# Hashed attention and a maxout feed-forward: the first batch's scores and transposes as products on 32 columns

## The chip, the cores and the metric

The kernel runs on one core of one Trainium2 chip. The metric is the device time of one execution in microseconds (us). The kernel before takes 295.62 us, the median of 3 runs (295.52 to 295.69).

## The reference

For each of 4 batches and 8 heads (768 positions, 64 dimensions), queries and keys are hashed to 6 sign bits with `proj`; a query attends only to keys of its own bucket; the result goes through a feed-forward layer that takes the maximum of three products.

```python
q_bits = (np.einsum('bhsd,dk->bhsk', q, proj) > 0)      # 6 bits, k likewise
mask = q_bucket[:, :, :, None] == k_bucket[:, :, None, :]
scores = np.where(mask, scale * (q @ k.T), -1e9)
attn = np.exp(scores - max) ; attn = attn / (attn.sum(-1) + 1e-9)
x = (attn @ v)                                          # to [3072 tokens, 512]
h = np.maximum(np.maximum(x @ w1, x @ w2), x @ w3)      # [3072, 768]
out = h @ w_out                                         # [3072, 512]
```

## The kernel before

**Units.** The 32 (batch, head) pairs are worked two heads at a time: 16 head pairs `pi`, 4 to a batch. A head pair has 12 units: 2 halves of the queries (`qh`, 384 each) times 3 parts of the keys (`kp`) times 2 heads. There are 192 units `u`, 48 to a batch (`UPB`), 6 to a query half (`UPG`), 12 to a head pair (`UPP`). The core's program is one loop over `u`; every engine gets its instructions in the order in which this loop issues them, and works them off in that order. Nothing is scheduled by a tool: the order is written out by hand.

**Preparing a head pair.** `prep_groups(pi)` gives four `tgroup`s, each of which turns one head of q or k round: three transposes of 128x128 fp32 on TensorE into the PSUM tile `mp` (L150), from where VectorE copies them to `T` (L158, L160) and, for pairs 2 to 7, the odd half of the positions also to `S` (L166, L168). Then `hashes` multiplies `T` with the projection (`bp`, L205: four fp32 products, each on 32 columns), VectorE makes bits of it (L208), and four small transfers on GpSimd's queue put the bits below the data in `S` (L214). `even` copies the other half (L217, GpSimd). So `S` has 70 rows, 64 of data and 6 of bits, and one product gives score and bucket match together. Pair 0 has its own path (`odd_first`, `hash_first`, `bits_first`), ordered by the list `first`. In the loop, a fill (one `tgroup` or one `hashes`) is issued at `u` = 2 to 6 and then at every odd `u` up to 60: 24 `tgroup`s of pairs 1 to 6, 6 `hashes`, and two `tgroup`s of pair 7.

**Scores.** `scores(u)` issues two products of 70 rows on 128 columns (keys) by 384 queries into `sc` (L301), which has two buffers, and ScalarE takes the exponential into one of 14 tiles `AT` (L304).

**Values.** `values_part` multiplies `AT` with `v` (`av`, L327, 8 products on 32 columns for one part of the keys) and with ones for the sums (`sm`, L332, 4 products on 32 columns). In the first batch one such group of 12 follows every second unit; `av` has one buffer. After a query half, `values` has VectorE take the result out (`sv`, `avs`, `ys`, L343 to L346).

**The chain of a head pair.** `normalize` collects the sums by a transfer (`dd`, SP queue, L367), inverts them on VectorE (`rr`, L370 and L372), writes them to DRAM (`rd`, SP queue, L373), reads them back spread over the partitions (`rb`, SP queue, L377), and multiplies on GpSimd into `xT` (L381). The list that it returns says how many units later each step is issued: invert, spread, scale. The steps wait in `steps` and are issued at the head of a loop body, in the order of their unit.

**Feed-forward.** `ffn_groups(b)` is issued from unit 13 of the next batch on (`FFN_AT`), about one group per unit: products with the weights (`l`, L244, four `jc` for the four head pairs of the batch), the maximum on VectorE (L249, L251), and the second product (L260). So the first batch, u = 0 to 60, has no feed-forward in it, and that of the last batch stands alone at the end of the program.

**Loads.** q and k of pair `pi + 2` are loaded when the preparation of `pi` begins, v of the next pair at the head of each pair (`load_v`, L122) and cast at its unit 10 (L125), weights in 15 parts at the units of `WEIGHTS_AT`, all on GpSimd's queue (L411 to L418).

Of the kernel before, what the change touches and what calls it, by code (L numbers as in the profile page):

```python
# [17 lines left out]
def kernel(  # L18
# [12 lines left out]
    nc = tc.nc  # L31
    B, H, S, D = q.shape
    NBITS = proj.shape[1]
    P = 128
    NCH = S // P

    HALF = S // 2
# [4 lines left out]
    NPAIR = B * HPAIR  # L42
# [10 lines left out]
    EPS = 2.0 ** -60  # L53

    AHEAD = 6
    ODD_LATE, ODD_PSUM = 1, 8
    LAG = 1

    konst = ctx.enter_context(tc.tile_pool(name="konst", bufs=1))
# [25 lines left out]

    def load_proj():
        for par in range(2):
            rows = slice(par * D, (par + 1) * D)
            nc.scalar.dma_start(pst[rows, :], proj[:, :])
            nc.vector.tensor_copy(pj[rows, 1 + par, 0:NBITS], pst[rows, :])  # L90
            nc.vector.tensor_copy(pj[rows, 0, par : 2 * NBITS : 2], pst[rows, :])

    bias_t = konst.tile([P, 1], FP32, name="bias_t")
    nc.vector.memset(bias_t[:], EXP_BIAS)
# [38 lines left out]
    def prep_groups(pi):  # L133
# [9 lines left out]
        def tgroup(side, hd):  # L143
            def go():
                if not st:
                    begin()
                mp = ms_ps.tile([P, 512], FP32, tag="ms", name="mp")
                n = natural[pi][side]
                for i in range(CH2):
                    nc.tensor.transpose(mp[:, i * P : (i + 1) * P], n[:, hd, 2 * i * D : (2 * i + 2) * D], iden[:])  # L150
                o = st["T2"][:, side, hd, :]
                if pi == 0 and (hd, side) != (0, 1):
                    if side == 0:
                        nc.scalar.mul(o, mp[:, 0:HALF], QS)
                    else:
                        nc.scalar.copy(o, mp[:, 0:HALF])
                elif side == 0:
                    nc.vector.tensor_scalar(out=o, in0=mp[:, 0:HALF], scalar1=QS, scalar2=None, op0=AluOp.mult)  # L158
                else:
                    nc.vector.tensor_copy(o, mp[:, 0:HALF])  # L160
                if pi == 0:
                    nc.gpsimd.tensor_copy(st["S"][0:D, side, hd, 0, :], o[0:D])
                elif ODD_LATE < pi < ODD_PSUM:
                    o, i_ = st["S"][0:D, side, hd, 1, :], mp[D : 2 * D, 0:HALF]
                    if side == 0:
                        nc.vector.tensor_scalar(out=o, in0=i_, scalar1=QS, scalar2=None, op0=AluOp.mult)  # L166
                    else:
                        nc.vector.tensor_copy(o, i_)  # L168
            return go
# [53 lines left out]
        if pi == 0:  # L223
            k0, k1 = (1, 0, 0, P), (1, 1, 0, P)
            early = (k0, k1, (0, 0, 0, HALF), (1, 0, P, HALF), (1, 1, P, HALF))
            return [tgroup(1, 0), tgroup(0, 0), tgroup(1, 1), lambda: odd_first(0), lambda: hash_first(0), tgroup(0, 1),
                    lambda: bits_first(0, early), lambda: scores(0), lambda: hash_first(1, (1,)), lambda: odd_first(1),
                    lambda: bits_first(1, early[:2]), lambda: scores(1), lambda: scores(2), lambda: hash_first(1, (0,)),
                    lambda: bits_first(1, early[2:]), lambda: bits_first(0, ((0, 1, 0, HALF),)),
                    lambda: bits_first(1, ((0, 1, 0, HALF),))]  # L230
        odds = [odd(1), odd(0)]
# [55 lines left out]
    UPB = NU // B  # L287
    UPG = NCH
    UPP = 2 * UPG
    WEIGHTS_AT = (2, 4, 6, 8) + tuple(range(12, 48, 5)) + (63, 67, 71)  # L290
    FFN_AT = 13
    FIRST = 2
    PAIRS_AT = UPB + UPP
# [2 lines left out]
    def scores(u):  # L296
        pi, qh, kp, hd = units[u]
        th = trans[pi]
        sc = sc_ps.tile([P, 2, 512], FP32, tag="sc", name="sc")
        for j in range(2):  # L300
            nc.tensor.matmul(sc[:, j, 0:HALF], th[0:KR, 1, hd, j, kp * P : (kp + 1) * P],  # L301
                             th[0:KR, 0, hd, qh, :], start=True, stop=True)
        at = at_tiles[u % NAT]
        nc.scalar.activation(at[:, :, 0:HALF], sc[:, :, 0:HALF], ActFn.Exp, bias=bias_t[:], scale=SCALE)  # L304

# [46 lines left out]
    def normalize(pi, q0, nq):  # L352
# [27 lines left out]
        def scale(i):  # L380
            return lambda: nc.gpsimd.tensor_mul(xt[:, jj, (q0 + i) * HALF : (q0 + i + 1) * HALF],  # L381
                                                avs[:, q0 + i, :], rb[:, i, :])

        gather()
        if nq == 1:
            return [(4, invert), (6, spread), (8, scale(0))] if pi == NPAIR - 1 else [(7, invert), (11, spread), (15, scale(0))]
        at = (8, 13, 18) if jj < 2 else (6, 9, 14)
        return [(at[0], invert), (at[1], spread)] + [(at[2], scale(i)) for i in range(nq)]

    with tc.manual_schedule():  # L390
# [6 lines left out]
        cast_v = {0: load_v(0, nc.sync)}  # L397
        load(2, nc.sync)
        first = prep_groups(0)
        for g in first:  # L400
            g()

        prep, hash_ready, late, ffn, steps = [], [], [], [], []
        f_credit = 0.0
# [3 lines left out]
        for u in range(NU):  # L408
            pi = units[u][0]
            b, ub = divmod(u, UPB)  # L410
            if u % UPP == 0 and pi + 1 < NPAIR:  # L411
                cast_v[pi + 1] = load_v(pi + 1, nc.gpsimd)
            if u == FIRST:
                cast_v[0]()
            if u % UPP == 10 and pi + 1 < NPAIR:
                cast_v[pi + 1]()
            if u in WEIGHTS_AT:
                nc.gpsimd.dma_start(*weight_parts.pop(0))  # L418
# [77 lines left out]
```

## Time and profile before

| What | us |
|---|---|
| Median of 3 runs | 295.62 |
| The profiled execution, its own time | 295.93 |
| Its span in the profile | 294.0 |
| TensorE (PE) busy | 285.0, 97% of the span |
| ScalarE (ACT) busy | 195.4, 66% |
| VectorE (DVE) busy | 188.7, 64% |
| GpSimd (POOL) busy | 139.7, 48% |
| Stretch from u = 8 to the feed-forward, 18.02 to 69.43: PE | 49.51 of 51.41 |
| Same stretch: ACT, DVE, POOL | 46.13, 40.44, 44.38 |

TensorE's products are pipelined: a product is shown for about 0.17 us longer than it keeps the next one from starting, and products on different groups of 32 columns run side by side. So a row such as "0.51 us, x8" is the time from the first start to the last end, and the cost of a group on the path is read from its start to the start of the next group. PEld is the loading of the stationary operand. The granted clock of TensorE is full nearly throughout.

### The profile page before, as it was taken

To read this page: it belongs to the slowest core of one execution; us is meant where nothing else is said; L and a number is where in the kernel's file an instruction comes from. 1 tells how busy PE (TensorE), PEld (TensorE's weight loads), DVE (VectorE), ACT (ScalarE), POOL (GpSimd) and SP (SyncE) were. 2 spreads that over 40 slices of the span, in tenths; PEclk is the share of its full clock that TensorE was granted. 3 is DMA by queue.
4 is the path that set the end of the run, shared out by engine and by line. 5 is a ranking of instruction groups with operands and counts; after the bars stand their busy time and mean duration, and the time that the engine had idled before them with its cause. 6 is when DMAs were issued, how large, how long until landed. Compare 5 with 4: busy or idle time off the path is not lost.

```text
span 294.0 us, 6792 instructions
## 1 busy us (share of the span) xinstructions
PE 285.0 (97%) x2592; PEld 159.7 (54%) x2592; DVE 188.7 (64%) x419; ACT 195.4 (66%) x238; POOL 139.7 (48%) x187
## 2 busy tenths in 40 slices
PE   8898999998999999999999999999999999999994
PEld 4454454444656566555665556555655555555551
DVE  2886977788865387736667377654757167657480
ACT  3779899886847956797785965888696956010202
POOL 2765799889806556291905636090801702220000
PEclk9999999999999999999999999999999999999999
DMA  6877666864952733336222522315011211230203
GB/s 206 266 166 204 164 169 186 233 161 123 271 158 63 233 97 116 107 67 261 83 88 64 176 107 59 101 48 175 9 54 59 102 49 41 64 134 2 107 0 108
DMA packets 20276, 35.90 MB, mean 122 GB/s; under 512 B 6080, under 2 KB 12484, under 8 KB 20244
## 3 DMA queue, kind: packets, MB, share of 16 engines
q0 software_dynamic: 8992, 19.81, 25.2%
q1 hardware_dynamic: 10948, 15.52, 16.3%
q8 instruction: 20, 0.33, 0.5%
q10 hardware_dynamic: 304, 0.13, 0.2%
q14 instruction: 12, 0.10, 0.1%
HBM read 31.46 MB, written 6.39 MB: 129 GB/s over the span
## 4 chain that ended last, share of the span: by engine, by line
PE 90%; DMA 3%; DVE 2%; ACT 2%; issue 1%; POOL 0%; SPq 0%; ACTq 0%; POOLq 0%; DVEq 0%
PE l L244 32%; PE sc L301 21%; PE av L327 11%; PE l L260 11%; PE mp L150 6%; PE sm L332 5%; PE bp L205 3%; DMA rb<-rd 2%; ACT AT L304 2%; PE wm L393 1%; PE bp L191 1%; DMA rd<-rr 0%; DVE S L168 0%; POOL xT L381 0%; DVE rr L372 0%
## 5 line engine op out<-in xcount | busy, mean ns | idle before, releaser
L304 ACT ACTIVATE AT<-sc,bias_t 128x768 f16<-128x768 f32 x192 | 168.9, 903 | 53.9 <-PE sc L301 48.3
L244 PE MATMUL l<-xT,w_sb 128*128 128x384 f16 x576 | 110.0, 326 | 1.0 <-POOL xT L381 1.0
L301 PE MATMUL sc<-S 70*128 70x384 bf16 x384 | 93.8, 327 | 1.8 <-ACT AT L304 1.5
L244 PEld LDWEIGHTS <-w_sb 128*128 128x128 f16 x576 | 55.9, 97 | 36.3 <-issue 1.5
L214 POOL DMA_DIRECT2D S<-bits x58 | 32.9, 570 | 86.0 <-DVE bits L208 55.5
L251 DVE TENSOR_TENSOR ht<-ht,l 128x384 f16<-128x384 f16 x96 | 52.9, 551 | 18.1 <-PE l L244 13.5
L301 PEld LDWEIGHTS <-S 70*128 70x128 bf16 x384 | 33.8, 98 | 41.7 <-issue 20.2
L327 PE MATMUL av<-AT,vo 128*32 128x385 f16 x768 | 48.3, 330 | 1.0 <-DVE avs L344 0.7
L381 POOL TENSOR_TENSOR xT<-avs,rb 128x384 f16<-128x384 f32 x32 | 31.5, 1000 | 31.1 <-DMA rb<-rd 31.1
L249 DVE CAST ht<-l 128x384 f16<-128x384 f32 x48 | 26.5, 553 | 25.3 <-PE l L244 24.4
L274 ACT COPY osb<-l 128x512 f32<-128x512 f32 x23 | 13.4, 585 | 35.0 <-PE l L260 35.0
L260 PE MATMUL l<-wout_sb,ht 128*128 128x512 f16 x144 | 36.5, 379 | 0.0
L332 PE MATMUL sm<-AT,ones 128*32 128x384 f16 x384 | 32.7, 324 | 0.0
L327 PEld LDWEIGHTS <-vo 128*32 128x32 f16 x768 | 17.3, 95 | 20.0 <-issue 10.9
L160 DVE COPY T<-mp 128x384 f32<-128x384 f32 x31 | 17.0, 549 | 13.7 <-PE mp L150 13.6
L158 DVE TENSOR_SCALAR T<-mp 128x384 f32<-128x384 f32 x30 | 16.6, 554 | 12.7 <-PE mp L150 11.3
L217 POOL CAST S<-T 64x1536 bf16<-64x1536 f32 x15 | 22.1, 1476 | 0.0
L260 PEld LDWEIGHTS <-ht 128*128 128x128 f16 x144 | 14.0, 97 | 12.7 <-DVE ht L251 0.2
L344 DVE TENSOR_SCALAR avs<-av,sv 128x384 f32<-128x384 f32 x32 | 19.8, 618 | 1.6
L346 DVE TENSOR_SCALAR ys<-sm 128x384 f32<-128x384 f32 x32 | 17.5, 548 | 0.0
L343 DVE TENSOR_SCALAR sv<-av 128x1 f32<-128x1 f32 x32 | 5.1, 158 | 18.3 <-PE av L327 17.8
L150 PE MATMUL mp<-iden,knat 128*128 128x128 f32 x96 | 16.2, 277 | 0.0
(45 smaller groups left out, 191.4 us busy)
## 6 DMA issues: line engine op xcount, KB each, us to landing
out_dram<-osb SPq DMA_DIRECT2D x23, 256.0 KB
vnat<-in_v_dram POOLq DMA_DIRECT2D x15, 384.0 KB, 4.8
knat<-in_k_dram POOLq DMA_DIRECT2D x13, 384.0 KB, 4.3
qnat<-in_q_dram POOLq DMA_DIRECT2D x13, 384.0 KB, 5.1
rb<-rd SPq DMA_DIRECT2D x24, 192.0 KB
w_sb<-in_moe_w_dram POOLq DMA_DIRECT2D x12, 192.0 KB, 4.7
rb<-rd SPq DMA_DIRECT2D x16, 96.0 KB
S<-bits POOLq DMA_DIRECT2D x58, 9.0 KB, 2.4
```

Source lines behind the costliest of these rows:

```text
L150: nc.tensor.transpose(mp[:, i * P : (i + 1) * P], n[:, hd, 2 * i * D : (2 * i + 2) * D], iden[:])
L214: eng.dma_start(st["S"][D:KR, side, hd, :, :], bits[p0 : p0 + 2 * NBITS, :])
L217: nc.gpsimd.tensor_copy(st["S"][0:D, :, :, 0, :], st["T2"][0:D])
L244: nc.tensor.matmul(ps[:, 0:HALF], w_sb[wi][:, jc, fb * P : (fb + 1) * P], xb[:, jc, hf * HALF : (hf + 1) * HALF], start=(jc == 0), stop=(j ...
L249: nc.vector.tensor_copy(hts[fb][:], ps[:, 0:HALF])
L251: nc.vector.tensor_tensor(out=hts[fb][:], in0=hts[fb][:], in1=ps[:, 0:HALF], op=AluOp.max)
L260: nc.tensor.matmul(st2["l2"][:, 0:DM], hts[fb][:, tb * P : (tb + 1) * P], wout_sb[:, fb, :], start=(fb == 0), stop=(fb == NFB - 1))
L301: nc.tensor.matmul(sc[:, j, 0:HALF], th[0:KR, 1, hd, j, kp * P : (kp + 1) * P], th[0:KR, 0, hd, qh, :], start=True, stop=True)
L304: nc.scalar.activation(at[:, :, 0:HALF], sc[:, :, 0:HALF], ActFn.Exp, bias=bias_t[:], scale=SCALE)
L327: nc.tensor.matmul(av[p0 : p0 + 32, 0 : HALF + 1], vones[pi][:, hd, d0 : d0 + 32], ats[hd][:, c % 2, 0 : HALF + 1], start=(c == 0), stop=( ...
L332: nc.tensor.matmul(sm[32 * t : 32 * t + 32, 0:HALF], ones[:, :], ats[hd][:, half, 0:HALF], start=(s == 0), stop=(s == CH2 - 1))
L381: return lambda: nc.gpsimd.tensor_mul(xt[:, jj, (q0 + i) * HALF : (q0 + i + 1) * HALF], avs[:, q0 + i, :], rb[:, i, :])
```

## The change

Four things change, and all but the last two bear on the first batch alone.

1. For u = 3 to 60, `scores` issues eight products on 32 columns each (`M = 32`) in place of two on 128: four groups of 32 keys, in four column groups, for each of the two halves.
2. For pairs 1 to 6 (`TILED` = 7), a `tgroup` issues twelve fp32 products with the identity, each of 32 columns by 128, in place of three transposes.
3. The chain of a pair: for the third pair of a batch the steps stand at 7, 11, 16 units in place of 6, 9, 14; for the fourth pair the scale stands at 14 in place of 15 (the last pair of all keeps 4, 6, 8).
4. Loads: v is loaded two pairs ahead, at unit 8 of a pair, and cast at unit 4 of the pair before its own (unit 10 at the start); the first 12 weight parts go out from unit 4 to 52 in place of 2 to 47. At the start, the second half of the copies of the projection moves behind the first `tgroup`, and one hash of pair 0 moves ahead of the scores of unit 2.

```diff
-    ODD_LATE, ODD_PSUM = 1, 8
+    ODD_LATE, ODD_PSUM, TILED = 1, 8, 7
...
     def load_proj():
         for par in range(2):
-            rows = slice(par * D, (par + 1) * D)
-            nc.scalar.dma_start(pst[rows, :], proj[:, :])
-            nc.vector.tensor_copy(pj[rows, 1 + par, 0:NBITS], pst[rows, :])
-            nc.vector.tensor_copy(pj[rows, 0, par : 2 * NBITS : 2], pst[rows, :])
+            nc.scalar.dma_start(pst[par * D : (par + 1) * D, :], proj[:, :])
+
+    def place_proj(par):
+        rows = slice(par * D, (par + 1) * D)
+        nc.vector.tensor_copy(pj[rows, 1 + par, 0:NBITS], pst[rows, :])
+        nc.vector.tensor_copy(pj[rows, 0, par : 2 * NBITS : 2], pst[rows, :])
...
                 for i in range(CH2):
-                    nc.tensor.transpose(mp[:, i * P : (i + 1) * P], n[:, hd, 2 * i * D : (2 * i + 2) * D], iden[:])
+                    if 0 < pi < TILED:
+                        for g in range(4):
+                            c0 = 2 * i * D + 32 * g
+                            nc.tensor.matmul(mp[32 * g : 32 * g + 32, i * P : (i + 1) * P], n[:, hd, c0 : c0 + 32],
+                                             iden[:], start=True, stop=True)
+                    else:
+                        nc.tensor.transpose(mp[:, i * P : (i + 1) * P], n[:, hd, 2 * i * D : (2 * i + 2) * D], iden[:])
...
-                    lambda: bits_first(1, early[:2]), lambda: scores(1), lambda: scores(2), lambda: hash_first(1, (0,)),
+                    lambda: bits_first(1, early[:2]), lambda: scores(1), lambda: hash_first(1, (0,)), lambda: scores(2),
...
-    WEIGHTS_AT = (2, 4, 6, 8) + tuple(range(12, 48, 5)) + (63, 67, 71)
+    WEIGHTS_AT = (4, 8, 13, 17, 21, 26, 30, 34, 39, 43, 47, 52, 63, 67, 71)
...
+        M = 32 if FIRST < u < UPB + FFN_AT else P
         for j in range(2):
-            nc.tensor.matmul(sc[:, j, 0:HALF], th[0:KR, 1, hd, j, kp * P : (kp + 1) * P],
-                             th[0:KR, 0, hd, qh, :], start=True, stop=True)
+            for p0 in range(0, P, M):
+                nc.tensor.matmul(sc[p0 : p0 + M, j, 0:HALF], th[0:KR, 1, hd, j, kp * P + p0 : kp * P + p0 + M],
+                                 th[0:KR, 0, hd, qh, :], start=True, stop=True)
...
-            return [(4, invert), (6, spread), (8, scale(0))] if pi == NPAIR - 1 else [(7, invert), (11, spread), (15, scale(0))]
-        at = (8, 13, 18) if jj < 2 else (6, 9, 14)
+            return [(4, invert), (6, spread), (8, scale(0))] if pi == NPAIR - 1 else [(7, invert), (11, spread), (14, scale(0))]
+        at = (8, 13, 18) if jj < 2 else (7, 11, 16)
...
         first = prep_groups(0)
-        for g in first:
+        place_proj(0)
+        for i, g in enumerate(first):
             g()
+            if i == 0:
+                place_proj(1)
...
-            if u % UPP == 0 and pi + 1 < NPAIR:
-                cast_v[pi + 1] = load_v(pi + 1, nc.gpsimd)
+            ahead = 1 if u == 0 else 2 if u % UPP == 8 else NPAIR
+            if pi + ahead < NPAIR:
+                cast_v[pi + ahead] = load_v(pi + ahead, nc.gpsimd)
             if u == FIRST:
                 cast_v[0]()
-            if u % UPP == 10 and pi + 1 < NPAIR:
+            if u % UPP == (4 if pi else 10) and pi + 1 < NPAIR:
                 cast_v[pi + 1]()
```

The text of the prediction counts lines by the kernel before.

## The prediction

> **What bounds the kernel now.** I read the page's busy times, the chain that ended last, the groups by line, and then the timeline of the first batch and of the tail.
>
> ```profile
> span 294.0 us, 6792 instructions
> PE 285.0 (97%) x2592; PEld 159.7 (54%) x2592; DVE 188.7 (64%) x419; ACT 195.4 (66%) x238; POOL 139.7 (48%) x187
> ...
> PE 90%; DMA 3%; DVE 2%; ACT 2%; issue 1%; POOL 0%; SPq 0%; ACTq 0%; POOLq 0%; DVEq 0%
> ...
> L301 PEld LDWEIGHTS <-S 70*128 70x128 bf16 x384 | 33.8, 98 | 41.7 <-issue 20.2
> ```
>
> PE bounds the program: 97% busy, 90% of the chain. What the change gains or loses in the first batch reaches the end, since from 71 to 259 us PE is never idle. The last line shows score weights idle for "issue" (20.2 us in 48 places): nothing that another engine did was missing. The timeline of PE shows where:
>
> ```profile
> 44.39 0.85 PE L205 MATMUL bp<-T,pj 128*32 128x384 f32 x8
> 45.18 0.50 PE L301 MATMUL sc<-S 70*128 70x384 bf16 x2
> 45.61 0.51 PE L327 MATMUL av<-AT,vo 128*32 128x385 f16 x8
> 45.95 0.34 PE L332 MATMUL sm<-AT,ones 128*32 128x384 f16 x4
> 46.22 0.50 PE L301 MATMUL sc<-S 70*128 70x384 bf16 x2
> 46.55 0.49 PE L150 MATMUL mp<-iden,knat 128*128 128x128 f32 x3
> 46.88 0.49 PE L301 MATMUL sc<-S 70*128 70x384 bf16 x2
> 47.30 0.51 PE L327 MATMUL av<-AT,vo 128*32 128x385 f16 x8
> ```
>
> From start to start: sc to mp 0.33, mp to sc 0.33, sc to av 0.42, av to sm 0.34, sm to sc 0.27. Four products side by side cost 0.16 to 0.17 a round (av: 2 rounds; three value groups in a row at 28.11, 28.61, 29.11 stand 0.49 apart). So each passage between 32 and 128 columns costs extra: sc to av 0.42-0.33 = 0.09, sm to sc 0.27-0.165 = 0.10, and the hash (0.79 for two passes of 0.33) about 0.1 at its end. ACT is close behind, 46.13 of 51.41 us, with 0.78 to 0.80 for one exponential when it is not kept waiting, against 1.69/2 = 0.85 per unit on PE.
>
> ```profile
> 51.79 0.44 DVE L372 RECIPROCAL rr<-rr 32x48 f32<-32x48 f32 x1
> ...
> 52.46 0.62 DVE L344 TENSOR_SCALAR avs<-av,sv 128x384 f32<-128x384 f32 x1
> ...
> 53.13 0.51 PE L327 MATMUL av<-AT,vo 128*32 128x385 f16 x8 [0.68 <-DVE avs L344]
> 53.45 0.55 DVE L158 TENSOR_SCALAR T<-mp 128x384 f32<-128x384 f32 x1
> ...
> 70.01 0.99 POOL L381 TENSOR_TENSOR xT<-avs,rb 128x384 f16<-128x384 f32 x1 [0.21 <-DMA rb<-rd]
> ...
> 71.05 1.62 PE L244 MATMUL l<-xT,w_sb 128*128 128x384 f16 x9 [0.97 <-POOL xT L381]
> ...
> 257.69 1.00 POOL L381 TENSOR_TENSOR xT<-avs,rb 128x384 f16<-128x384 f32 x1 [3.66 <-DMA rb<-rd]
> ...
> 258.74 1.46 PE L244 MATMUL l<-xT,w_sb 128*128 128x384 f16 x8
> ```
>
> PE's real waits: values wait for DVE, which does the inversion first (0.68); the first feed-forward product waits for xT (0.97); and in the tail xT of the last pair is done at 258.69, 0.05 before its product.
>
> **Part 1, scores on 32 columns.** Eight products in four column groups are two rounds of 0.164 = 0.33, as now. The passages go. Between u = 3 and 60 stand 26 value groups and 6 hashes, one hash beside values: 31 islands, 62 passages of 0.095 = 5.9 us. The two transposes of pair 7 bring 4 back (-0.4). Gain 5.5.
>
> **Part 2, transposes as products.** fp32 products make two passes each. Nearest row: the first hash, 8 products of 384 (4 passes of two groups) in 1.48 us of busy time; less the 0.17 that the last is shown too long, 0.33 a pass, or 0.109 for 128 columns. Twelve products in four groups are 3 x 2 passes = 0.66 against 0.33 now. From below, the streaming alone: the hash's pass after the first, 0.32/3 x 6 = 0.64. From above: the first pass of a hash is 0.347, so 0.027 of weights can stand open; were that so each time, 6 x 0.027 = 0.16 more, 0.82. I take 0.66, because the middle passes of the first hash (6.68 to 7.00, 7.00 to 7.32) show no opening. 24 x 0.33 = 7.9 us lost.
>
> The two parts meet in the cycle of two units: now 1.69, then 4 rounds of scores 0.66, values 0.49, turn 0.66 = 1.81. With a hash: now 2.25 (43.97 to 46.22), then 0.66+0.49+0.65 = 1.80. Ten units hold four of one and one of the other: 4 x 0.11 - 0.45 = 0.0. So the steady stretch comes out even, and the waits decide. ACT needs 1.6 for two units and does not bind.
>
> **Part 3, the waits of the steady stretch.** From u = 20 (29.70) to u = 60 (67.07) 37.37 us pass; 16 cycles of 1.69 and 4 of 2.25 are 36.1, so 1.3 are waits (avs 0.86 and 0.16, vo 0.3 at 59.13). After: 15 x 1.81 + 4 x 1.80 + one cycle of pair 7 at 1.69 = 36.0. The invert of the third pair moves behind the take-out, so avs come in time; but then DVE does `rr` (0.7) before the copy T of the last turn, and the hash waits for that copy. Counted from the end of the turn before the take-out: T, S at +0.2 and +0.77, sv +1.25, avs +1.45, ys +1.98, rr +2.44, T +3.18 to +3.74. PE stands at the hash at 1.81+0.33+0.49+0.33 = 2.96: 0.83 lost. The same order costs 0.2 at the hash of u = 35. So the wait changes its place and 1.0 of 1.3 remains; with vo cast a pair earlier its wait goes. 36.0 + 1.0 = 37.0: gain 0.4.
>
> **Part 4, before that.** The hash of unit 0's pair moved ahead lets u = 3 start at 11.67 (now 12.04): bits at 11.06 to 11.6 in place of 11.39 to 11.94. Then four turns stand between scores: 4 x 0.33 + 4 x 0.66 = 3.95, the last ends at 15.62 (now about 15.0), its copy at 16.38, the hash 17.09, nine rounds of values 18.57: u = 8 starts 0.55 later than now (18.02). ACT hides nothing of it: PE was already the later one at the hash. From there to u = 20 stand 12 scores, 6 value groups, 5 turns and a hash: 10.2 us now with 10 passages, 10.9 after. Waits are now 11.68-10.2 = 1.5 (twice 0.40 on ACT), after 0.7 (ACT 0.3, the hash on T behind a take-out 0.4): 11.6. So +0.5 at u = 20, +0.1 at u = 60. `place_proj(1)` moves two copies of 0.16 behind the first T; they end at 6.27, before PE reaches the hash at 6.33: nothing; if the cover goes, at most 0.3.
>
> **Part 5, the feed-forward's start.** PE needs the fourth pair's xT at 69.43 + 0.49 + 0.1 = 70.0. GpSimd: the four S transfers of pair 6 end at 68.33 as now, then the v load (0.72; v moved, it now stands ahead), and xT, ahead of the cast of S (1.48) in the new order because scale is issued at 14: 69.05 to 70.05. The spread has to land by 69.05; now it lands at 69.9 after an issue at 62.03, with the loads of k, q (61.01, 61.74) and v (62.46) in flight. In the new order a weight part of half v's size stands there instead. Bounds: 5.1 us as for the spread issued at 48.71 (in time), and 7.84 as now (no gain). I take landing at 69: l goes on at 70.1 in place of 71.05, gain 0.95 with the 0.1 of part 4 in it. On SP's queue the fourth pair's collection (1.18) now stands ahead of the third pair's `rd`; its spread was in by 63.20, when GpSimd reached it, so 0.5 later is covered. On GpSimd's queue two weight issues (0.59 each) leave the first ten us; S there waits for DVE anyway (3.31 at 17.52). Weight parts 5 units later: the last leaves at about 63, lands in 4.7 (its row), and is first needed at 71.9: covered.
>
> **Part 6, the tail.** With 16 in place of 14 the scale of pair 14 falls behind that of pair 15 on GpSimd (196 against 194). That one waits for a spread landing at 257.69 and takes 1.0; then pair 14's first half needs 1.0: 259.69. PE needs it as third `jc` at 258.74 + 2 x 0.16 = 259.07: 0.68 lost at the end. Bounds: 0 if the spread of pair 15 lands 0.7 earlier, 1.0 if the loop's end moves too.
>
> **Sum** against the profiled execution (295.93; 294.0 span and 1.93 around it): the first feed-forward product goes on 0.95 earlier, the +0.1 of parts 1 to 4 in it, and the tail gives back 0.68: -0.3. The median of the runs is 0.31 lower than the profiled one: 295.62 - 0.3 = 295.3.
>
> [...] On the path of issue: cycles of two units would hold 16+12+24 = 52 products with their weights in place of 19. The densest stretch now, 28.11 to 29.60, passes 36 of them at 0.041 us each without a gap.
>
> [...]
>
> **The rivals.**
> - *Faster: DVE is not late.* If the copies T come in time (hashes at 6, 15, 35, 45: 0.5+0.4+0.2+0.8), the gain is 1.9 more: 293.4. For it: DVE has 40.4 us of work in 51.4. Against: it works in order, and its order puts take-outs ahead of T. Chance 0.28.
> - *Slower: the fp32 products pay for their weights.* 0.16 more in each of 24 turns: +3.9, 299.2. Against: the middle passes of the first hash; for it: 128 columns stream in a third of the time that covered the weights there. It turns the sign to a measurable loss from 0.04 a turn. Chance 0.20.
> - *Slower: PE's issue binds.* At 0.041 a product the cycle is 2.13, +0.32 in some 24: +8, 303. The densest stretch is limited by the array, so that is the upper end. Chance 0.04.
> - *The passages stay*, because they come from rows or types and not from columns: +5.5, 301. Against: av to sm, and hash to values at 16.1, pass without a gap. Chance 0.05.
>
> **How the numbers follow.** The forecast, 295.3, has 0.43; its own range is 294.4 to 296.2 (landing and tail by their bounds). A measurement tells about 0.2%, 0.6 us: of the 0.43, 0.15 are faster, 0.20 the same, 0.08 slower. Faster: 0.15+0.28 = 0.43. Slower: 0.08+0.20+0.04+0.05 = 0.37. Range: down to 293.4 and up to 299.2 leaves out about half of the last two cases and the edges of the first two.
>
> **What would show it.** Score rows "70*32" x8, 0.33 from start to start; no "issue" before scores in 12 to 67 us; turns x24 at 0.66 (0.82 is the second rival); u = 60 at about 67.2; l at 70.1 without a wait on xT; in the tail xT of pair 15 alone, then two, and PE idle 0.7. Wrong would make it a turn far from 0.66, or hashes that do not wait for T.

## The result and the profile after

The changed kernel takes 297.37 us (median of 7 runs, 296.97 to 298.02), the kernel before, run beside it, 295.69 (7 runs, 295.46 to 296.78): a ratio of 1.0054, 95% interval [1.0037, 1.0070]. It is 1.7 us slower. The forecast was 295.3, 0.3 faster, so the direction was wrong; the time lies inside the range. The profiled execution took 297.33 (before 295.93) and has a span of 295.5 (before 294.0). Here and below, a median is that of all executions, while a ratio leaves out those more than 1.5% above the fastest of their kernel.

As in the prediction, a turn is the products of one `tgroup`, the take-out is what VectorE does with the values (`sv`, `avs`, `ys`), the collection is the transfer `dd`, and the spread is the transfer `rb`.

The page of the changed kernel: busy times, the chain that ended last by engine, and the group of the score weights (busy us, mean ns, then the idle time before them and what ended it).

```profile
span 295.5 us, 8499 instructions
...
PE 288.7 (98%) x3444; PEld 176.2 (60%) x3444; DVE 189.2 (64%) x419; ACT 196.6 (67%) x238; POOL 139.4 (47%) x187
...
PE 89%; DMA 4%; DVE 2%; ACT 1%; POOL 1%; issue 1%; SPq 1%; POOLq 0%; ACTq 0%; DVEq 0%
...
L311 PEld LDWEIGHTS <-S 70*32 70x32 bf16 (+1 forms) x732 | 41.3, 97 | 32.5 <-issue 10.2
```

The idle time put down to "issue" before score weights has halved, from 20.2 to 10.2 us. On the page alone the change looks as if it had worked. What it cost is in the stages. The timeline of PE in the steady stretch shows the cycle of two units:

```profile
48.29 0.61 PE L337 MATMUL av<-AT,vo 128*32 128x385 f16 x8
...
48.62 0.44 PE L342 MATMUL sm<-AT,ones 128*32 128x384 f16 x4
...
48.78 0.61 PE L311 MATMUL sc<-S 70*32 70x384 bf16 x8
...
49.11 0.93 PE L155 MATMUL mp<-iden,qnat 128*32 128x128 f32 x23
...
50.10 0.61 PE L337 MATMUL av<-AT,vo 128*32 128x385 f16 x8
```

From start to start: av to sm 0.33, sm to sc 0.16 (0.27 before), sc to mp 0.33; the next scores start at 49.77, so a turn of fp32 products costs 0.66, and from av to av are 1.81 us. Each of these is what the forecast took. So the prices on the array were right, and the time went elsewhere. The start of the last score product of some units, in us from the start of the span:

| Point | before | after | difference | forecast |
|---|---|---|---|---|
| u = 3 | 12.20 | 11.82 | -0.38 | -0.37 |
| u = 8 | 18.19 | 18.76 | +0.57 | +0.55 |
| u = 20 | 29.87 | 30.58 | +0.71 | +0.5 |
| u = 60 | 67.25 | 68.42 | +1.17 | +0.1 |
| feed-forward goes on after its wait for xT | 71.05 | 71.91 | +0.86 | -0.95 |
| u = 65 | 74.64 | 75.65 | +1.02 | -0.95 |
| end of the span | 294.0 | 295.5 | +1.5 | -0.3 |

From u = 63 to the tail the difference doesn't move. Two places hold the error: u = 20 to 60, and the feed-forward's start. The timeline of the changed kernel around the hash of u = 45 and at the feed-forward's start:

```profile
53.95 0.51 PE L337 MATMUL av<-AT,vo 128*32 128x385 f16 x8
...
54.27 0.24 DVE L380 TENSOR_REDUCE rr<-dd 32x48 f32<-32x96 f32 x1
...
54.54 0.44 DVE L382 RECIPROCAL rr<-rr 32x48 f32<-32x48 f32 x1
...
54.91 0.48 DVE L166 TENSOR_SCALAR T<-mp 128x384 f32<-128x384 f32 x1
...
55.45 0.12 PEld L213 LDWEIGHTS bp<-T,pj 128*32 128x32 f32 x3 [0.56 <-DVE T L166]
...
70.87 0.99 POOL L391 TENSOR_TENSOR xT<-avs,rb 128x384 f16<-128x384 f32 x1 [0.26 <-DMA rb<-rd]
...
71.91 0.49 PE L252 MATMUL l<-xT,w_sb 128*128 128x384 f16 x2 [0.51 <-POOL xT L391]
```

VectorE inverts (0.7 us) before it makes the copy T that the hash needs, and the hash stands for it; xT comes at 71.86, because its spread landed at 70.8 and not at 69. And the tail:

```profile
258.60 2.90 POOL L391 TENSOR_TENSOR xT<-avs,rb 128x384 f16<-128x384 f32 x3 [11.18 <-DMA rb<-rd]
...
259.75 0.49 PE L252 MATMUL l<-xT,w_sb 128*128 128x384 f16 x2
...
260.59 3.57 PE L252 MATMUL l<-xT,w_sb 128*128 128x384 f16 x21 [0.35 <-POOL xT L391]
```

The scales of pairs 14 and 15 stand in one row of three, PE gets through two products and waits: 0.5 us lost here (+1.02 becomes +1.5), 0.68 forecast.

### The profile page after: what moved, and what is told of

Its sections match the earlier page's. It is cut to its first block, busy times and chain, and to the rows that moved or that the text cites. A ratio compares the mean times of both kernels' runs of the same rounds, so it can differ in the third digit from the quotient of the medians.

```text
span 295.5 us, 8499 instructions
## 1 busy us (share of the span) xinstructions
PE 288.7 (98%) x3444; PEld 176.2 (60%) x3444; DVE 189.2 (64%) x419; ACT 196.6 (67%) x238; POOL 139.4 (47%) x187
## 4 chain that ended last, share of the span: by engine, by line
PE 89%; DMA 4%; DVE 2%; ACT 1%; POOL 1%; issue 1%; SPq 1%; POOLq 0%; ACTq 0%; DVEq 0%
PE l L252 31%; PE sc L311 20%; PE av L337 11%; PE l L268 9%; PE sm L342 5%; PE mp L155 4%; PE mp L158 4%; PE bp L213 4%; DMA rb<-rd 3%; PE wm L403 1%; PE bp L199 1%; POOL xT L391 1%; ACT AT L314 1%; DMA rd<-rr 1%; DVE S L204 0%
## 5 line engine op out<-in xcount | busy, mean ns | idle before, releaser
L311 PE MATMUL sc<-S 70*32 70x384 bf16 (+1 forms) x732 | 100.2, 326 | 0.7 <-DVE S L204 0.5
L311 PEld LDWEIGHTS <-S 70*32 70x32 bf16 (+1 forms) x732 | 41.3, 97 | 32.5 <-issue 10.2
L337 PE MATMUL av<-AT,vo 128*32 128x385 f16 x768 | 50.7, 329 | 0.2
L342 PE MATMUL sm<-AT,ones 128*32 128x384 f16 x384 | 34.7, 324 | 0.0
L337 PEld LDWEIGHTS <-vo 128*32 128x32 f16 x768 | 20.5, 95 | 14.7 <-issue 5.2
L168 DVE COPY T<-mp 128x384 f32<-128x384 f32 x31 | 16.9, 545 | 15.5 <-PE mp L158 10.2
L342 PEld LDWEIGHTS <-ones 128*32 128x32 f16 x384 | 11.5, 98 | 5.1
```

The source lines that it names most:

```text
L311: nc.tensor.matmul(sc[p0 : p0 + M, j, 0:HALF], th[0:KR, 1, hd, j, kp * P + p0 : kp * P + p0 + M], th[0:KR, 0, hd, qh, :], start=True, stop ...
L337: nc.tensor.matmul(av[p0 : p0 + 32, 0 : HALF + 1], vones[pi][:, hd, d0 : d0 + 32], ats[hd][:, c % 2, 0 : HALF + 1], start=(c == 0), stop=( ...
L342: nc.tensor.matmul(sm[32 * t : 32 * t + 32, 0:HALF], ones[:, :], ats[hd][:, half, 0:HALF], start=(s == 0), stop=(s == CH2 - 1))
```

## The experiments

The theories. **A:** on the array the tiled products are even in the steady cycle; the loss is the turns ahead of u = 20 (+0.7), VectorE that comes late with T and with the take-outs, and the tail. **B:** the products on 32 columns cost it by themselves. **C:** the moved chains and loads cost it. Kernels whose names begin with the same letter ran on one chip beside the kernel before (the repetition of y1 by itself); ratios are against that one. The kernel before has medians from 295.69 to 296.28 on the chips of these runs, so what a stage costs is read from the traces, and whether it is faster from the ratios.

### The halves of the change

u1, the changed kernel with the chain of the last two pairs at its old place:

```diff
-        at = (8, 13, 18) if jj < 2 else (7, 11, 16)
+        at = (8, 13, 18) if jj < 2 else (7, 11, 16) if pi < NPAIR - 2 else (6, 9, 14)
```

> The changed kernel with the last batch's third pair (pair 14) put back to 6, 9, 14. Theory A (the loss is: turns before u = 20, copies and take-outs that come late on VectorE, and the order of xT in the tail): the end comes 0.5 us earlier than in the changed kernel (PE waited 0.35 at 260.59 and started its last feed-forward 0.5 later), so 296.9, and nothing before u = 180 moves. Rival B (the products on 32 columns cost it all): the same time as the changed kernel.

Measured 297.54, ratio 1.0026 [1.0000, 1.0051]. In its trace the difference to the kernel before is +1.29 at u = 65 and +1.3 at the end of the span, so nothing is lost in the tail any more:

```profile
259.01 0.99 POOL L391 TENSOR_TENSOR xT<-avs,rb 128x384 f16<-128x384 f32 x1 [3.69 <-DMA rb<-rd]
...
260.03 3.25 PE L252 MATMUL l<-xT,w_sb 128*128 128x384 f16 x19
```

The 0.5 of the tail is shown. In this execution 0.3 of it was lost ahead of the tail, 0.1 at the start and 0.2 in a longer wait at xT.

u2, the kernel before with the tiled scores and turns alone, and u3, the changed kernel without them (`TILED` = 1, `M = P`):

> The kernel before with the products on 32 columns alone (scores and turns), chains, loads and start as before. Theory A: a cycle of two units 1.81 us, u = 8 some 0.95 late, u = 60 1.2 to 1.8 late, no loss in the tail, the kernel 1.0 to 1.6 above the one before. Rival B (products cost more than passages give: 7.9 - 5.5): 2.4 above. Rival C (the moved chains and loads make the loss): within 0.3 of the kernel before.

> The changed kernel with transposes and scores on 128 columns as before: only chains, loads and start are moved. Theory A: start 0.35 earlier, the wait on v gone (0.3), the tail 0.5 later: within 0.4 of the kernel before. Rival B: 0.8 below it. Rival C: 1.5 above it.

u2: 298.24, ratio 1.0065 [1.0031, 1.0100]. u3: 296.0, ratio 0.9991 [0.9962, 1.0021]. So C falls, and the tiled products carry the loss. u2 is 2.1 above the kernel before, between the 1.0 to 1.6 of theory A and the 2.4 of theory B, so its time doesn't decide between them. The trace of u2 tells where it went: against the kernel before -0.24 at u = 3, +0.71 at u = 8, +0.85 at u = 20, +1.95 at u = 60, +2.11 at u = 65. That is 0.95 in the first four turns, 0.14 up to u = 20 and 1.1 in the stretch that the forecast had as even, some 0.5 of it at u = 52, a wait for v's cast (the step is 1.61, and 1.12 in the changed kernel, whose cast is earlier).

u4, the changed kernel with tiled scores and plain transposes:

> The changed kernel with transposes as before and scores on 32 columns. Each of 26 turns now stands between two passages, so of 62 passages only 10 go: 1.0 us below the run with chains, loads and start alone, if passages are what they cost (0.095 each) and the wait is PE's; the same as that run, if what passes away is refilled by waits for VectorE. Against the changed kernel: 24 x 0.33 - 48 x 0.095 = 3.4 below by PE's sum; 1 to 2 below if waits hide part of it.

Measured 296.66, ratio 0.9998 [0.9969, 1.0027], 0.7 above u3 and not 1.0 below it. Its profiled execution had a lowered granted clock (0.982) and isn't read. w4 below comes back to it.

### VectorE: a copy taken off it

v1, the changed kernel with the last copy T of a pair on ScalarE:

```diff
+                elif side == 0 and hd == 1 and 1 < pi < ODD_PSUM:
+                    nc.scalar.mul(o, mp[:, 0:HALF], QS)
                 elif side == 0:
                     nc.vector.tensor_scalar(out=o, in0=mp[:, 0:HALF], scalar1=QS, scalar2=None, op0=AluOp.mult)
```

> The changed kernel, with the last copy T of each pair from the third to the eighth on ScalarE in place of VectorE (same size, 128x384). Theory A (the tiled products are even in the steady cycle; what was lost there is that VectorE is late with T and with the take-outs): from u=20 to u=60 37.84 us become 36.7 to 37.2, the hash of u=45 no longer waits 0.69 for T, the waits for avs (about 1.0 in five places) shrink by half; at the end 0.3 to 0.9 us of it remain, since the first feed-forward product then stands at xT. Theory B (the products on 32 columns themselves cost it): 37.8 as before, time the same within 0.2 us.

Measured 297.2, ratio 1.0055 [1.0034, 1.0075]: no gain that the time can tell. The trace shows the mechanism and its size. From u = 20 to u = 60 37.26 us pass, where the changed kernel took 37.84 and theory B had no gain, and the hash of u = 45 no longer stands:

```profile
53.29 0.48 ACT L166 ACTIVATE T<-mp 128x384 f32<-128x384 f32 x1
53.32 0.12 PEld L339 LDWEIGHTS <-vo 128*32 128x32 f16 x8 [0.34 <-DVE avs L356]
...
53.65 0.23 DVE L382 TENSOR_REDUCE rr<-dd 32x48 f32<-32x96 f32 x1
...
54.15 0.82 PE L215 MATMUL bp<-T,pj 128*32 128x384 f32 x8
```

ScalarE makes T from 53.29 on, while VectorE is still at the take-out and the inversion, and the hash follows the scores without a gap. The wait for avs in the second line stays, though, and with it 1.2 us of such waits in the stretch (1.0 in the changed kernel): that half of the expectation was missed. At xT PE then waits 0.65 in place of 0.51, but from u = 62 to u = 63 pass 3.43 us in both kernels, so nothing is given back there: counted from u = 3, v1 is 0.67 ahead of the changed kernel at u = 65. The wait:

```profile
69.55 0.65 PE L254 MATMUL l<-xT,w_sb 128*128 128x384 f16 x3
69.78 1.02 POOL L393 TENSOR_TENSOR xT<-avs,rb 128x384 f16<-128x384 f32 x1
...
70.85 1.31 PE L254 MATMUL l<-xT,w_sb 128*128 128x384 f16 x7 [0.65 <-POOL xT L393]
```

### The fourth pair's chain, earlier

v2, the changed kernel with another chain for the fourth pair; v3, the same with copy and tail; v4, v3 without the tiled products:

```diff
-... else [(7, invert), (11, spread), (14, scale(0))]
+... else [(5, invert), (8, spread), (14, scale(0))]
```

> The changed kernel, with the inversion of the batch's last pair at 5 in place of 7 and its spread at 8 in place of 11. Theory A: its rr and rd then stand ahead of the second half's collection on SyncE's queue, the spread is issued some 2.5 us earlier (62 in place of 64.4) and lands by 69 in place of 70.8, xT is there before PE, the wait of 0.51 for xT goes, the first feed-forward product starts 0.4 to 0.6 earlier, and so does the end. Rival: the transfer is held by the loads of k, q and weights in flight, it lands at 70.5 as before, nothing is gained; or rr, now ahead of a copy T, makes a hash wait 0.4 more.

> The changed kernel with three things: last copy T of a pair on ScalarE, the earlier chain of the fourth pair (5, 8), and the old places of the chain for the last two pairs (6, 9, 14). Theory A: 0.7 in the steady stretch, 0.5 at the feed-forward's start, 0.5 in the tail: 1.2 to 1.8 us less than the changed kernel, within 0.3 us of the kernel before. Theory B: only the 0.5 of the tail.

> The same three things, with scores on 128 columns and transposes as before (no products on 32 columns but the old ones). Theory A: the waits on VectorE stand here too (1.27 us from u=20 to u=60 in the kernel before), so they shrink by 0.5 to 0.9, the tail gives nothing or 0.5: 0.5 to 1.5 us under the kernel before, and 0 to 0.6 under the run with the tiled products. Theory B: 2.0 under the run with the tiled products.

All three were misses, in the same way. v2: 299.31, ratio 1.0124 [1.0103, 1.0145]. v3: 298.24, 1.0106 [1.0064, 1.0147]. v4: 297.89, 1.0075 [1.0057, 1.0094]. The timeline of v2 and of v4, the first half's inversion and the values behind it:

```profile
58.94 0.19 DVE L380 TENSOR_REDUCE rr<-dd 32x24 f32<-32x48 f32 x1 [1.35 <-DMA dd<-ys]
...
60.67 0.62 DVE L354 TENSOR_SCALAR avs<-av,sv 128x384 f32<-128x384 f32 x1
...
61.43 0.51 PE L337 MATMUL av<-AT,vo 128*32 128x385 f16 x8 [0.52 <-DVE avs L354]
```

```profile
56.96 0.19 DVE L382 TENSOR_REDUCE rr<-dd 32x24 f32<-32x48 f32 x1 [2.71 <-DMA dd<-ys]
...
59.45 0.66 PE L339 MATMUL av<-AT,vo 128*32 128x385 f16 x8 [2.00 <-DVE avs L356]
```

VectorE reaches the inversion before the denominators have been collected and stands for the transfer, 1.35 and 2.71 us; the take-out is behind it in its order, and PE's values behind the take-out. The collection is issued at 55.06 in v2 and is there at 58.9. In v4, whose array is the earlier one, VectorE is there sooner and stands longer: 1.4 us ahead of the kernel before at u = 51, it is 1.9 behind at u = 54. Of these 3.3 us, 2.1 are the standstill (the step to u = 52); the other 1.1 fall into the two steps behind it, when PE's granted clock was half, from 59.69 to 63.10. So the 297.89 of v4 is not the price of the wait alone: all four of its executions have a mean clock of 0.993 or 0.994.

w2 moves the inversion of the first half alone, by one unit (6, 10, 14), with copy and tail; w3 is w2 without the tiled products, w4 w2 with tiled scores and plain transposes, w1 the changed kernel itself beside them:

> The changed kernel itself once more, as the neighbour of the next three on this chip: 1.3 to 1.9 us above the kernel before. Its trace says how much the start (first score of u=3) differs from one execution to another.

> The changed kernel with the last copy T of a pair on ScalarE, with the last two pairs' chain at 6, 9, 14, and with the inversion of the first half of a batch's last pair one unit earlier (6, spread at 10). Theory (two units earlier VectorE stood 1.35 to 2.7 us for the collection of the denominators, which had not landed): one unit earlier it has landed, or lacks at most 0.4 us, and rd leaves before the second half's collection. Then 0.6 in the steady stretch, 0.3 to 0.5 at the feed-forward's start and 0.5 in the tail: 1.0 to 1.6 us under the changed kernel. Rival: VectorE still stands for the collection by 1 us or more, and the time is above that of the copy's move alone.

> The same, with scores on 128 columns and plain transposes. Theory: the moved chains and loads are worth 0 to 0.6, the copy's move 0.6, the tail's old places 0 to 0.5: 0.6 to 1.6 us under the kernel before, so faster than both. Rival: the waits fill again somewhere else (at xT before the feed-forward), within 0.3 us of the kernel before.

> The same, with scores on 32 columns and plain transposes. By the array's sum a cycle of two units is then 4 x 0.165 + 0.49 + 0.33 + 2 x 0.095 = 1.67 (1.69 with 128 columns) and one with a hash 1.80 (2.25): 2 us under the run without the tiled scores. Rival: ScalarE, with 1.6 us of exponentials in each cycle, or VectorE binds instead, and it ends within 0.5 us of that run, on either side.

w1: 297.61, ratio 1.0045 [1.0030, 1.0059]; from u = 3 to u = 65 it loses 1.36 us against the kernel before, as the first execution did (1.40). w2: 297.18, 1.0034 [1.0019, 1.0049], 0.4 under w1 where 1.0 to 1.6 was expected. Its timeline:

```profile
58.40 0.19 DVE L382 TENSOR_REDUCE rr<-dd 32x24 f32<-32x48 f32 x1
...
58.62 0.29 DVE L384 RECIPROCAL rr<-rr 32x24 f32<-32x24 f32 x1
...
58.94 0.16 DVE L355 TENSOR_SCALAR sv<-av 128x1 f32<-128x1 f32 x1
59.14 0.62 DVE L356 TENSOR_SCALAR avs<-av,sv 128x384 f32<-128x384 f32 x1
...
59.90 0.51 PE L339 MATMUL av<-AT,vo 128*32 128x385 f16 x8 [0.73 <-DVE avs L356]
```

The collection is there now, but one unit earlier the inversion stands ahead of the take-out of u = 47 instead of behind it, and its 0.5 us go straight to PE: the step to u = 52 takes 1.73 in place of 1.12. The spread gained little: `rd` left at 59.95 and not 61.97, but the spread could be issued only at 64.21. So 7 was the better place. w3: 295.72, 0.9985 [0.9966, 1.0003], which can't be told from the kernel before; 0.6 to 1.6 less was expected. Its step to u = 52 takes 1.93 (1.40 in the kernel before), and its first feed-forward product waits 1.27 for xT.

w4: 297.68, 1.0040 [1.0009, 1.0072]. In its trace VectorE still stands 1.11 us for the collection at the moved inversion, PE 1.68 behind it, and then the granted clock is half from 61.75 to 68.58; so only the stretch before is read, and the ratio doesn't price the tiled scores. Its five executions with a mean clock of 0.998 or more took 295.2 to 296.9; those of w3, but for one, took 294.5 to 297.1. From u = 20 to 45 it needs 22.35 us, w3 22.24. A unit with a plain turn between tiled scores takes 0.91, and the cycle 1.73, where the sum of the array had 1.67: the passages that leave the values come back at the turn, and cost 0.06 more. The expected gain of 2 us was not there. The rival, within 0.5 of w3, fits the stretch; which engine holds it back was not tried.

### What reaches the end

x1 is u3 with copy and tail (chain at 7); x2 the changed kernel with copy and tail; x3 is x2 with the second pair's turns plain and scores on 128 columns up to u = 7:

```diff
-                    if 0 < pi < TILED:
+                    if 1 < pi < TILED:
...
-        M = 32 if FIRST < u < UPB + FFN_AT else P
+        M = 32 if 7 < u < UPB + FFN_AT else P
```

> Scores on 128 columns and plain transposes, with the moved chains, loads and hash of the change, the last copy T of a pair on ScalarE, the last two pairs' chain at 6, 9, 14; the batch's last pair inverted at 7 as in the changed kernel. Theory (VectorE's lateness is the loss that remains, and VectorE must not reach the inversion before the collection has landed): the wait at u=52 is 0.3 in place of 1.2, the first feed-forward product starts 1.0 to 1.5 us earlier than in the kernel before; 0.8 to 1.6 us under the kernel before, faster than both. Rival: it stands at xT for as much as it came earlier, within 0.4 us of the kernel before.

> The changed kernel with the last copy T of a pair on ScalarE and the last two pairs' chain at 6, 9, 14. Theory: the two gains add, 0.5 at the feed-forward's start and 0.5 in the tail: 0.8 to 1.1 us under the changed kernel, so 0.2 to 0.8 above the kernel before. Rival: one of them is taken back at xT: 0.5 under the changed kernel.

> The run with copy and tail, with the second pair's four transposes plain and the scores up to u=7 on 128 columns. Theory (a turn of fp32 products costs 0.33 more, and beside scores alone nothing comes back for it): u=8 starts 1.3 us earlier than with the fp32 products (4 x 0.33), of which ScalarE takes back 0.4 (0.79 for an exponential against 0.66 on the array), so 0.9; from there the spacing is the same; at the end 0.6 to 0.9 less. Rival (the first hash or xT takes it back): less than 0.3 at the end.

x2: 297.46 (296.97 without two executions of 302.75 and 429.01), ratio 1.0034 [1.0001, 1.0067]; in its trace +0.24 at u = 65 and 294.3 of span, 1.5 under w1's, of which 0.4 is an earlier start (u = 3 at 11.67 and 12.04). Copy and tail add, as theory A had it, in the trace; the other ten executions spread from 296.3 to 300.0, so the time shows less. x3: 295.9, 0.9997 [0.9970, 1.0024]. From u = 3 to u = 8 5.90 us pass, 6.94 in x2: 1.04 for four turns, 0.9 expected. x3 started 0.8 later than x2, so the spans are alike (294.4), and at xT it had its own wait of 0.2 more. x1: 295.39, 0.9974 [0.9945, 1.0003], 0.7 under the kernel before, between its theory (0.8 to 1.6) and its rival (0.4); at u = 62 it is 1.28 ahead of the kernel before, and gives 0.69 back at once:

```profile
68.15 0.65 PE L254 MATMUL l<-xT,w_sb 128*128 128x384 f16 x3
...
69.42 0.98 POOL L393 TENSOR_TENSOR xT<-avs,rb 128x384 f16<-128x384 f32 x1 [0.70 <-DMA rb<-rd]
...
70.46 0.81 PE L254 MATMUL l<-xT,w_sb 128*128 128x384 f16 x4 [1.66 <-POOL xT L393]
```

The chain of x1 has the reason, a spread of 6 us behind `rd` of 2.2. Loads of k and q and two weight parts were issued from 60.45 to 63.8:

```profile
60.52 2.17 DMA rd<-rr
...
63.27 6.01 DMA rb<-rd
```

x1 against x3 also prices the tiled products with the copy off VectorE: from u = 8 to u = 62 x1 gains 0.92 on the kernel before, x3 loses 0.09. In that form they cost 1.0: 0.33 up to u = 20, where the forecast's own sum had 0.7 more on the array, 0.14 behind u = 60, and 0.53 from u = 20 to u = 60, where its sum is even. There it is 36.74 against 37.27, and the waits for avs are the difference: at u = 28, 34, 46, 52 and 58 0.28, 0.15, 0.14, 0.31 and 0.35 above the cycle in x3; in x1 0.03, 0.12, 0.12, 0.27 and 0.10. Only u = 28 and u = 58 differ by more than 0.04. There the take-out stands beside a hash. The hash of u = 57 and the values behind it, in x3 and in x1:

```profile
63.63 0.83 PE L215 MATMUL bp<-T,pj 128*32 128x384 f32 x8
...
64.97 0.51 PE L339 MATMUL av<-AT,vo 128*32 128x385 f16 x8 [0.17 <-DVE avs L356]
```

```profile
62.17 0.85 PE L215 MATMUL bp<-T,pj 128*32 128x384 f32 x8
...
63.49 0.51 PE L339 MATMUL av<-AT,vo 128*32 128x385 f16 x8
```

The values start 1.34 us behind the hash's start in x3 and 1.32 in x1, because avs ends there 1.28 and 1.27 behind it. On the array they could have started at 0.65+0.33 = 0.98 in x3 and at 0.79+0.42 = 1.21 in x1. So the passages saved at this hash, 0.23 us, turn into a wait for VectorE. At u = 28 it is the same, 1.27 and 1.24.

### A version faster than both

y1 is x1, and y2 is x3, with the weight parts earlier:

```diff
-    WEIGHTS_AT = (4, 8, 13, 17, 21, 26, 30, 34, 39, 43, 47, 52, 63, 67, 71)
+    WEIGHTS_AT = (4, 6, 8, 11, 13, 17, 20, 24, 28, 32, 36, 40, 63, 67, 71)
```

> Scores on 128 columns, plain transposes, the change's chains, loads and hash, the copy on ScalarE, the old chain of the last two pairs, and the weight parts issued earlier (the last but three at u=40 in place of 52), so that none stands ahead of the spread that the first feed-forward product waits for. Theory (that spread took 6.0 us behind loads of k, q and two weight parts, and xT came 1.0 late): without 0.4 MB of weights in flight it takes 4 to 5 us, the wait for xT is 0 to 0.4, the product starts 0.6 to 1.0 earlier: 1.2 to 1.9 us under the kernel before. Rival: the weights in the earlier stretch delay k, q, v or other spreads by as much; then no change against the run without it (0.7 under the kernel before).

> The same with the tiled products from the third pair on (scores on 32 columns from u=8). Theory (tiled and plain are even in the steady cycle, what is left of the loss is VectorE and the second pair's turns): 0.5 to 1.2 us above the run with plain products, so 0 to 1.2 us under the kernel before. Rival (the tiled products cost by themselves): 2 us above it.

> The same kernel once more, for an undisturbed execution and a second interval: 0.8 to 1.6 us under the kernel before; in its trace u=63 starts 3.36 us after u=62 (no wait for xT), 1.2 to 1.6 us earlier than in the kernel before.

y1: 294.82, ratio 0.9961 [0.9941, 0.9981]. y1 again: 294.74, ratio 0.9955 [0.9938, 0.9971]. Faster than the kernel before and than the changed one, by 1.3 us and some 2.7. In the second execution (span 292.3) u = 3 is 0.57 ahead of the kernel before, u = 20 to 60 takes 36.74 (37.37 before), and from u = 62 to 63 pass 3.36 (3.74 before): it stands 1.82 ahead at u = 65. One execution of each series took much longer, 299.57 and 298.94. The first of them was profiled: PE stood 2.2 us for a hash's bits (from 43.05 to 45.27), and then the granted clock was half for 6.8 us. The wait for xT that is left in the second execution:

```profile
67.99 1.03 POOL L393 TENSOR_TENSOR xT<-avs,rb 128x384 f16<-128x384 f32 x1
...
69.08 1.77 PE L254 MATMUL l<-xT,w_sb 128*128 128x384 f16 x9 [0.44 <-POOL xT L393]
```

The row of xT names no spread any more: GpSimd comes to it without a gap from its other work.

y2: 297.65, ratio 1.0037 [1.0022, 1.0051], 2.8 above y1, and not 0.5 to 1.2 as theory A had it, nor the 2 of its rival. Its trace loses at three places where the other tiled kernels lose nothing. The timeline of y2 at the second and longest:

```profile
51.47 0.51 PE L313 MATMUL sc<-S 70*32 70x384 bf16 x7
51.74 0.56 DVE L170 COPY T<-mp 128x384 f32<-128x384 f32 x1 [0.68 <-PE mp L155]
...
52.31 0.56 DVE L178 CAST S<-mp 64x384 bf16<-64x384 f32 x1
...
53.06 0.09 PEld L313 LDWEIGHTS <-S 70*32 70x32 bf16 x1 [1.47 <-issue]
53.06 0.34 PE L313 MATMUL sc<-S 70*32 70x384 bf16 x1 [1.08 <-issue]
```

PE stops after seven of the eight products of one score tile, where the trace shows nothing that it waits for, and goes on 1.4 us later. The section on the hardware says what the trace shows of it. So y2 tells of something other than theory A, and its price isn't the price of the tiled products alone.

## Why the prediction was wrong, step by step

- **The array's prices (parts 1 and 2): right.** Passages 0.1, a turn 0.66 (24 records for its twelve fp32 products, 8 for the four of a hash: the two passes that the forecast counted), the cycle 1.81 (forecast 1.81), the unit with a hash 0.97. (The forecast's 4 x 0.11 is 4 x 0.12 by its own 1.69 and 1.81, 0.04 in ten units.) The rival of the weights (0.82 a turn) and that of the passages that stay are refuted by these rows. The rival of issue is refuted for this kernel: 24 products pass in the 0.66 of a turn, 0.027 each, and the cycle is 1.81, not 2.13.
- **Part 3, the steady stretch: the step that failed.** The forecast had 37.0 us with 1.0 of waits; 37.84 it was, with 1.8. The waits for T were as forecast: 0.69 at the hash of u = 45 (0.83) and 0.10 at that of u = 35 (0.2), and v1 showed them by taking that copy away. Wrong was the sentence that the avs "come in time": at u = 28, 34, 46, 52 and 58 PE waited for them, 1.0 in all. The term mis-sized is VectorE's chain after a turn. At u = 46, counted from the end of a turn (51.58), T began at +0.34 and not +0.2, S at +0.91 and not +0.77, `sv` at +1.50 and not +1.25, `avs` at +1.70 and not +1.45; PE wanted the values at +2.14, and got them at +2.37. The forecast had a margin of less than 0.1 there and gave it no price. At u = 28 and u = 58 the chain runs beside a hash, and part of what the array gained at that hash went into the wait, as x3 and x1 show. The forecast had counted the 0.45 of each hash as gained.
- **Part 4, before that: nearly right.** u = 3 and u = 8 to 0.02, u = 20 0.2 later than forecast. x3 showed the four turns at 1.04.
- **Part 5, the feed-forward's start: the second step that failed.** The forecast took a spread that lands at 69; it landed at 70.8. Its transfer took 6.4 us, between the bounds of 5.1 and 7.84. But the forecast had kept the old time of issue, 62.03, and it was issued at 64.42: `rd` left at 61.97 (60.65 before), as late as the array and VectorE by then were, since the chain is laid out by units, and 2.4 us lay between `rd` and the spread where there had been 1.4. PE itself came 1.1 later, by part 3. So there was no gain of 0.95 but a loss of 0.86. x1 and y1 show the other half: two weight parts fewer in flight, and the wait at xT falls from 1.66 to 0.44.
- **Part 6, the tail: right,** 0.5 for 0.68, and u1 took it away.

So from -0.3 to the +1.5 of the spans: 0.2 up to u = 20, 0.9 in the steady stretch, 0.7 of xT's landing beyond that, 0.2 in the first units after it, and 0.2 back in the tail. The rival on the faster side, in which VectorE isn't late, was the wrong way round: VectorE was late in more places than forecast.

With the copy off VectorE the waits for avs are still 1.23 in x3 and 0.64 in x1; 0.49 of this difference is the two places beside a hash. What stays open is how much of the spread of the tiled kernels' times is the stop that y2 shows.

## What to carry to other kernels

Where the sum on the bound engine comes out even, as it did here, the result hangs on the engines beside it (1.8 of waits in the 37.84 us of the steady stretch): write their chain out by starts and ends from rows of the trace, and price a thin margin as a wait: here one of less than 0.1 us became a wait of 0.23. A saving right ahead of a place where the chain binds can be lost there, as the 0.23 us at the hash of u = 57 was. A step that reads a transfer, put earlier in the order of a busy engine, can make everything behind it wait for that transfer (VectorE stood 1.35 us in v2 and 2.71 in v4); look for the landing first, and for what the step jumps over. A saving on the array can be lost again where the array needs the next transfer (x1 was 1.28 us ahead at u = 62 and gave 0.69 back at xT), so look at what is queued in front of it.

## What the runs showed of the hardware

**In y2 PE stopped three times with nothing in the trace to wait for.** The queue that the page lists as q8, kind "instruction", moves packets of 16 KB: 20 in the kernel before, whose trace has 5256 records of PE (2592 products, as many weight loads, 72 waits), and 27 in the changed one, which has 6960, so one for 263 and 258 records. In the first 55 us the kernel before has 4 of these packets, the changed one 9. In y2 PE stops at the records numbered 1473, 1985 and 2497 (counted from 0), 512 apart, in the midst of products for which the trace shows no wait. Each time it goes on 1.3 to 1.4 us after a packet of that queue has landed:

```
packet    start   landed   PE goes on   PE's record
#5        39.90   40.85    42.27        1473
#7        50.68   51.62    53.06        1985
#9        61.04   62.00    63.29        2497
```

The stops cost 0.7 at u = 33, 1.4 at u = 43 and 0.4 at u = 54, by the steps of these units against those of x3. The profiled executions of the changed kernel (9 packets in its first 55 us), v1 and x2 have no such stop. The author reads the stops as PE running out of instructions; the trace shows the stops, 2.5 us in all, and the packets. By the table, two packets go with 512 records. An estimate from that: if packet #5 brings the 256 records from 1473 on, and the others those before and behind them in turn, then up to 70 us PE starts a packet's records 1.2 to 3.8 us after it has landed in y2, 1.9 to 4.2 in the changed kernel, and 9.0 to 10.4 in y1's second execution. Counted like this, the tiled kernels have little in hand. Why the stop comes in y2, and whether loads in flight delay the packet, was not tried.

**Products started out of their order of issue.** In the changed kernel, when T was late for the hash, nothing started between 55.10 and 55.45. Once T was there, two score products (55.47 and 55.65) started before the last three products of the hash (55.80 to 55.81), and a values product beside those (55.81), though all three were issued behind the hash. So the order of issue didn't hold from one product to the next here. The author's reading is that a group of 32 columns that had its hash products behind it went ahead of the others; which group a product is on, the rows don't say:

```profile
55.47 0.50 PE L311 MATMUL sc<-S 70*32 70x384 bf16 x2
...
55.80 0.49 PE L213 MATMUL bp<-T,pj 128*32 128x384 f32 x2
...
55.81 0.33 PE L337 MATMUL av<-AT,vo 128*32 128x385 f16 x1
55.81 0.49 PE L213 MATMUL bp<-T,pj 128*32 128x384 f32 x1
```

**Four stretches at a granted clock of 0.5 came behind a standstill of PE.** Four profiled executions have one in their midst: v4 (3.4 us), w4 (6.8), y1's first (6.8) and u4 (10.2). Each began 0.06 to 1.6 us after PE had stood, for 2.0, 1.7, 2.2 and 1.2 us. Five other standstills of 1.2 to 1.8 us, one of them in x1, brought no such stretch. What decides was not tried.

**The start scatters.** With the same instructions, the last score product of u = 3 started between 11.29 (v1) and 12.52 (v2). In u3, with the same first instructions, two casts of VectorE (64x384, fp32 to bf16) took 1.23 and 0.97 us where the changed kernel's took 0.38 and 0.35, and u = 3 came at 13.41; one of those of v2 took 0.97 too. Why wasn't tried. For differences under 1 us, the stages are better compared from a common unit on than from the start of the span.
